# Set attention and a 2048-wide hard-swish layer on one core: the layer as a pairwise quadratic form over 32 inducing points

## The chip, the cores and the metric

The kernel runs on one core of a Trainium2 chip. The metric is device time in microseconds from the first to the last instruction of the program, as the median of three runs. Engines are named as in the profile: PE is TensorE's products and PEld its weight loads, DVE is VectorE, ACT is ScalarE, POOL is GpSimd, SP is SyncE.

## What is computed

Four batches of 12480 tokens of 128 features, 32 inducing points, and a layer that is 2048 wide:

```
def mab(q, kv):
    s = scale * (q @ kv.transpose(0, 2, 1))
    s = s - s.max(-1, keepdims=True)
    a = np.exp(s)
    a /= a.sum(-1, keepdims=True) + 1e-09
    return a @ kv
h = mab(I, x)                 # I: the 32 inducing points; h: (4, 32, 128)
attn = mab(x, h)              # (4, 12480, 128), reshaped to (49920, 128)
h2 = attn @ w_in              # (49920, 2048)
g = h2 * np.clip(h2 + 3.0, 0.0, 6.0) / 6.0
out = g @ w_out               # (49920, 128)
```

Where no entry of `h2` is beyond 3 in size, the clip does nothing and `g` is `h2*h2/6 + h2/2`. Each row of `attn` is a mean of the 32 rows of `h` with weights `a` that sum to one. So the square part of `out` is a quadratic form in the 32 weights.

## The kernel before, in words

Tokens go in chunks of 512 (24 full ones and one of 192 per batch). Before the first batch, and then woven into the chunks of the batch ahead, **phase A** makes `h`: x is cast to bf16 by a DMA into DRAM (`xbf`, L135) and read back transposed (`xt`, L139); per group of four 128-token tiles the fp32 rows come in again (`xs`, L182), are cast to fp32r on VectorE (`xa_ring`, L193), scores are taken (`s1p`, L196), exponentiated on ScalarE (`a`, L203), and four products add to `Hnd` (L166).

A chunk then runs in steps. **S1a** takes the scores of tokens against `h` (`s2p`, L244) and their exponentials; **S1b** sums, inverts and scales them on VectorE (L275 to L282) and transposes them (`a2tp`, L307); **S1c** multiplies by `H_sb` (`otu`, L321) and makes an fp32r copy `OT` (ScalarE, L323) and a bf16 copy `OTb` (VectorE, L325). **S2** is the layer: the linear half as one product with a folded 128x128 matrix (`W_sb`, L334), and for each of 16 blocks of 128 hidden units a product `hp` (L354), a square, and a product that adds to `outTp` (L344). Ten of the squares are one ScalarE instruction (L361), six are a copy and a product on VectorE (L364, L365); the second product of a block runs three blocks behind the first.

**S3** copies `outTp` (L374), transposes it back (`fp`, L387), copies it out of PSUM (L389, L391) and stores it (L394, L402). The order of the work comes from the order of the code, from `hooks` that put S1b, S1c, S3 and phase A of the next batch between the blocks j of S2, and from the buffers of the pools. x, weights and results move on SP's queue, the DMA cast on POOL's, `w_out` on ACT's.

## Time and profile before

| | |
|---|---|
| median of 3 runs | 1231.09 us (1230.43 to 1231.32) |
| span of the profiled execution | 1230.7 us, 0.4 us under the median |
| PE busy | 1034.0 us, 84% of the span |
| DVE busy | 844.4 us, 69% |
| ACT busy | 701.1 us, 57% |
| POOL busy | 6.7 us, 1% |
| moved by DMA | 79.86 MB, 65 GB/s over the span |
| granted TensorE clock | 0.962 of full, over the span |

The profiled execution has its span as its own time. A busy time is the union of an engine's instructions over the whole span, so it mixes the stages: the first 92 us, in which x and the weights arrive, the first aggregation up to about 162 us, and four batches of about 267 us each. What a stage is bound by is read from that stage alone. PE's products are pipelined: each record lasts longer than the distance to the next start, and the distance is what the engine spends.

### The profile page before, as it was taken

The page shows a single profiled execution, that of the slowest core. Times are in us where ns is not written, and L with a number is a line of the kernel's source. Part 1 is how long each engine was busy: PE and PEld are TensorE (multiplying, and loading weights), DVE is VectorE, ACT ScalarE, POOL GpSimd, SP SyncE. Part 2 cuts the span into 40 slices and gives each one's busy share as a digit, 9 for nine tenths or more (in the row PEclk, how much of TensorE's full clock was granted, in tenths as well). Part 3 has the DMA queues.
Part 4 walks back from the last instruction along what each step waited for, and adds up shares of the span by engine and source line. Part 5 has one row for each costly group of instructions (what it writes and reads, how often), then busy time and mean ns, then how long its engine had stood idle before and what let it go on. Part 6 is the DMA issues. An engine that isn't in the chain of part 4 may idle for free.

```text
span 1230.7 us, 16661 instructions
## 1 busy us (share of the span) xinstructions
PE 1034.0 (84%) x5413; PEld 455.1 (37%) x5413; DVE 844.4 (69%) x2342; ACT 701.1 (57%) x1614; POOL 6.7 (1%) x18
## 2 busy tenths in 40 slices
PE   0034699999999899999999799999999899999997
PEld 0033334444434434344434344334444333333333
DVE  0112578777778677788777677778876677777776
ACT  0011266666666466666666466666667466666665
POOL 2000000000000000000000000000000000000000
PEclk9995599999999899999999899999999899999999
DMA  9997311112113411112114311112110000000001
GB/s 229 218 226 182 98 35 44 52 52 60 43 47 82 112 44 43 52 44 61 52 47 109 76 44 52 48 48 60 44 38 26 14 25 26 27 26 27 20 25 38
DMA packets 155238, 79.86 MB, mean 65 GB/s; under 512 B 53872, under 2 KB 153744, under 8 KB 154256
## 3 DMA queue, kind: packets, MB, share of 16 engines
q1 hardware_dynamic: 153664, 64.98, 19.5%
q0 software_dynamic: 960, 12.78, 4.9%
q8 instruction: 42, 0.69, 0.3%
q10 hardware_dynamic: 528, 1.05, 0.2%
q14 instruction: 44, 0.36, 0.1%
HBM read 53.23 MB, written 38.34 MB: 74 GB/s over the span
## 4 chain that ended last, share of the span: by engine, by line
PE 45%; DVE 26%; issue 13%; DMA 7%; ACT 4%; SPq 4%; ACTq 0%; DVEq 0%; POOL 0%; POOLq 0%
PE outTp L344 21%; DVE u L364 16%; PE hp L354 16%; DVE q L365 7%; DMA xbf<-in_x_dram 4%; ACT q L361 4%; SPq L139 4%; PE otu L321 3%; DMA xs<-in_x_dram 2%; PE a2tp L307 2%; DVE rr L275 1%; PE fp L387 1%; DVE ri L281 1%; DMA out_dram<-ostage 1%; DVE xa_ring L193 0%
## 5 line engine op out<-in xcount | busy, mean ns | idle before, releaser
L354 PE MATMUL hp<-OTb,w_in_bf 128*128 128x512 bf16 (+1 forms) x1600 | 570.4, 379 | 46.9 <-DVE u L364 36.5
L361 ACT ACTIVATE q<-hp 128x512 bf16<-128x512 f32 (+1 forms) x1000 | 533.3, 618 | 89.7 <-PE hp L354 81.0
L344 PE MATMUL outTp<-q,w_bf 128*128 128x512 bf16 (+1 forms) x1600 | 549.3, 375 | 12.6
L364 DVE CAST u<-hp 128x512 bf16<-128x512 f32 x600 | 387.6, 666 | 14.4 <-PE hp L354 14.4
L365 DVE TENSOR_TENSOR q<-u 128x512 bf16<-128x512 bf16 x600 | 221.7, 408 | 0.8
L344 PEld LDWEIGHTS <-w_bf 128*128 128x128 bf16 x1600 | 141.6, 98 | 167.8 <-issue 91.0
L354 PEld LDWEIGHTS <-w_in_bf 128*128 128x128 bf16 x1600 | 145.9, 97 | 146.2 <-issue 91.0
L389 DVE COPY ostage<-fp 128x128 f32<-128x128 f32 x196 | 55.0, 281 | 181.4 <-PE fp L387 175.5
L323 ACT CAST OT<-otu 128x512 fp32r<-128x512 f32 (+1 forms) x100 | 57.5, 575 | 198.7 <-PE otu L321 198.7
L387 PE MATMUL fp<-ident_r,oT 128*128 128x128 f32 x392 | 126.2, 322 | 16.3 <-DVE ostage L389 5.0
L203 ACT ACTIVATE a<-s1p 128x128 fp32r<-128x128 f32 x96 | 26.6, 277 | 175.6 <-PE s1p L196 143.6
L166 PE MATMUL Hnd<-xa_ring,a 128*32 128x130 f32 x392 | 88.5, 312 | 31.3 <-DVE xa_ring L193 30.1
L325 DVE CAST OTb<-otu 128x512 bf16<-128x512 f32 (+1 forms) x100 | 67.6, 676 | 64.0 <-ACT OT L323 63.8
L193 DVE CAST xa_ring<-xs 128x128 fp32r<-128x128 f32 x392 | 61.3, 212 | 72.5 <-DMA xs<-in_x_dram 69.7
L387 PEld LDWEIGHTS fp<-ident_r,oT 128*128 128x128 f32 x392 | 54.6, 139 | 121.4 <-DVE ostage L389 46.2
L374 ACT CAST oT<-outTp 128x512 fp32r<-128x512 f32 (+1 forms) x100 | 57.5, 575 | 31.1 <-PE outTp L344 31.1
L391 ACT COPY ostage<-fp 128x128 f32<-128x128 f32 (+1 forms) x196 | 65.6, 335 | 8.8 <-PE fp L387 8.8
L313 DVE CAST a2t<-a2tp 32x512 fp32r<-32x512 f32 (+1 forms) x100 | 65.9, 659 | 0.0
L166 PEld LDWEIGHTS Hnd<-xa_ring,a 128*32 128x32 f32 x392 | 43.7, 116 | 52.0 <-DVE xa_ring L193 33.5
L196 PE MATMUL s1p<-I_T_bf,xt 128*128 128x32 bf16 x392 | 27.1, 183 | 34.3 <-DMA xt<-xbf 30.1
L334 PE MATMUL outTp<-OT,W_sb 128*128 128x512 f32 (+1 forms) x100 | 50.7, 507 | 2.4 <-ACT OT L323 1.6
L307 PEld LDWEIGHTS a2tp<-ident_r,a2n 128*32 128x32 f32 x392 | 25.3, 98 | 71.8 <-DVE a2n L282 65.2
(46 smaller groups left out, 351.1 us busy)
## 6 DMA issues: line engine op xcount, KB each, us to landing
xs<-in_x_dram SPq DMA_DIRECT2D x96, 256.0 KB, 2.9
out_dram<-ostage SPq DMA_DIRECT2D x96, 256.0 KB, 2.3
xbf<-in_x_dram POOLq DMA_DIRECT2D x12, 1040.0 KB, 37.1
w_in_f<-in_moe_w_in_dram SPq DMA_DIRECT2D x1, 1024.0 KB, 6.6
xs<-in_x_dram SPq DMA_DIRECT2D x4, 64.0 KB, 1.9
out_dram<-ostage SPq DMA_DIRECT2D x4, 64.0 KB, 2.3
xt<-xbf SPq DMA_TRANSPOSE x12, 7.5
xs<-in_x_dram SPq DMA_DIRECT2D x4, 32.0 KB, 2.0
```

The source lines that it names most:

```text
L166: nc.tensor.matmul(Hnd[:Mi, : C + 2], lhsT=p_a1[:rows, i * Mi : (i + 1) * Mi], rhs=xa_ring[:rows, slot, : C + 2], start=(t == 0), stop=(t ...
L193: nc.vector.tensor_copy(xa_ring[:rows, slot, :C], xs[:rows, i, :C])
L313: nc.vector.tensor_copy(a2t[:Mi, :ntok], a2tp[:Mi, :ntok])
L323: nc.scalar.copy(OT[:, :ntok], otu[:, :ntok])
L325: nc.vector.tensor_copy(OTb[:, :ntok], otu[:, :ntok])
L344: nc.tensor.matmul(outTp[:, :ntok], lhsT=w6_bf[:, j, :], rhs=qs[j][:, :ntok], start=False, stop=(j == FB - 1),)
L354: nc.tensor.matmul(hp[:, :ntok], lhsT=w_in_bf[:, j * P : (j + 1) * P], rhs=OTb[:, :ntok],)
L361: nc.scalar.activation(q[:, :ntok], hp[:, :ntok], ACT.Square)
L364: nc.vector.tensor_copy(u[:, :ntok], hp[:, :ntok])
L365: nc.vector.tensor_mul(q[:, :ntok], u[:, :ntok], u[:, :ntok])
L387: nc.tensor.transpose(fp[:rows, :C], oT[:, r0 : r0 + rows], ident_r[:, :])
L391: nc.scalar.copy(ostage[:rows, sl, :], fp[:rows, :C])
```

## The change

The whole kernel is written anew. With the clip inactive, the square part is rewritten with the identity that for weights of sum one the square of a mean is the mean of the squares less the sum over pairs of `a_i a_j (G_i - G_j)^2`, G being `w_in` applied to the rows of `h`. What is left per token is a product with 32 exact values of the layer at the inducing points, and one with a coefficient for each of the pairs; the products of exponentials `e_i e_j` are made as `exp` of sums of scores.

- A batch is cut into six groups of 2048 tokens and one of 192 (`groups`; 16 tokens to a partition, or 4 to each of 48 partitions), a group into chunks of 512 tokens. x is loaded as `xr` (fp32r) and, from the second batch on, again as `xb` (bf16), both on POOL's queue (`load_x`); in batch 0 VectorE and ScalarE cast it.
- **A** (`a_T`, `a_s1`, `a_agg`): transposes on TensorE through one PSUM buffer `pt`, scores, exponentials, `hnd` and the running sums `dacc`.
- **C** (`c_head` to `c_tail`), once a batch: `h` and its shifted sums and differences (`W`, `dH`), the layer at the inducing points (`c_G`, `c_L`, giving `BD`), and the pair coefficients `Cq` from 16 difference products and their squares (`c_sq`).
- **B**, per chunk: three base products and exponentials (`b_base`), three products of them on VectorE (`b_prod`), one fp32r and sixteen bf16 products into `op` (`b_out`), scaled by the squared inverse row sum into `os` (`b_evac`). Per group: `b_e`, `b_f`, `b_r` make the exponentials, the row sums and `r_all`.
- The order is the order of the code (`manual_schedule`): step t issues the base products of chunk t + 2 and the output of chunk t; A of the next batch is spread over the first 16 steps of a batch, C over the next six.
- At the end five counts test the largest `G`, the row sums and the sums of the weights; one number `bad_i` is loaded by every engine, and a branch goes to `direct_path`, which does the whole computation again token by token in 96-row tiles (three loops of 130 passes in each of four batches), or past it.

The diff, cut to what the steps below speak of (all functions shown above are taken out, `direct_path` is not shown):

```diff
-ACT_SQ_BLOCKS = 10
-MM2_DEPTH = 3
...
+        psF = es.enter_context(tc.tile_pool(name="psF", bufs=3, space=PSUM))
+        psO = es.enter_context(tc.tile_pool(name="psO", bufs=2, space=PSUM))
+        psX = es.enter_context(tc.tile_pool(name="psX", bufs=1, space=PSUM))
+        psS = es.enter_context(tc.tile_pool(name="psS", bufs=1, space=PSUM))
+        psH = es.enter_context(tc.tile_pool(name="psH", bufs=1, space=PSUM))
...
+        def load_x(b, g):
+            t0, p, n = groups[g]
+            src = x[b, t0 : t0 + p * n, :].rearrange("(p i) c -> p i c", i=n)
+            t = xin.tile([P, TG, C], FP32R, name="xr")
+            nc.gpsimd.dma_start(t[:p, :n, :], src)
+            xs[(b, g)] = t
+            if b > 0:
+                tb = xbin.tile([P, TG, C], BF16, name="xb")
+                nc.gpsimd.dma_start(tb[:p, :n, :], src)
+                xbs[(b, g)] = tb
...
+            pt = psX.tile([P, 1024], BF16, name="pt")
+            for i in range(lo, hi):
+                nc.tensor.transpose(pt[:, (i - lo) * p : (i - lo + 1) * p], xb[:p, i, :], ident_b[:p, :p])
+            nc.vector.tensor_copy(st["xT"][:, t0 + lo * p : t0 + hi * p], pt[:, : (hi - lo) * p])
...
+            s1 = psS.tile([P, 512], FP32, name="s1", tag="s1")
+            for i in range(n):
+                nc.tensor.matmul(
+                    s1[:p, i * M : (i + 1) * M],
+                    lhsT=st["xT"][:, t0 + i * p : t0 + (i + 1) * p],
+                    rhs=I_T[:, :],
+                )
+            a1 = a1p.tile([P, TG * M], FP32R, name="a1")
+            nc.scalar.activation(a1[:p, : n * M], s1[:p, : n * M], ACT.Exp, scale=scale)
...
+                nc.tensor.matmul(
+                    st["hnd"][:M, :C],
+                    lhsT=a1[:p, i * M : (i + 1) * M],
+                    rhs=xs[(b, g)][:p, i, :],
+                    start=(g == 0 and i == 0),
...
+                ahead = 3 if b == 0 else 2
+                if g + ahead < NGR:
+                    load_x(b, g + ahead)
...
+            dps = psF.tile([P, 512], FP32, name="dps", tag="fb")
+            nc.tensor.matmul(dps[:M, :2], lhsT=dred[:, :], rhs=ones[:, :2])
+            nc.vector.tensor_copy(d_all[:M, b : b + 1], dps[:M, :1])
...
+            gp = psF.tile([P, 512], FP32, name="gp", tag="fb")
+            for jb in range(FB):
+                nc.tensor.matmul(
+                    gp[:, jb * M : (jb + 1) * M],
+                    lhsT=w_in_r[:, jb * P : (jb + 1) * P],
+                    rhs=st["HTr"][:, :],
+                )
+            r6 = cst.tile([P, 512], FP32, name="r6")
+            nc.vector.tensor_scalar(r6[:, :], gp[:, :], 3.0, 0.0, op0=ALU.add, op1=ALU.max)
+            hs = cst.tile([P, FB, M], FP32R, name="hs")
+            nc.vector.scalar_tensor_tensor(
+                hs[:, :, :].rearrange("p a m -> p (a m)"), r6[:, :], 6.0, gp[:, :], op0=ALU.min, op1=ALU.mult
+            )
+            nc.vector.tensor_reduce(
+                g_all[:, b : b + 1], gp[:, :], axis=AX.X, op=ALU.max, apply_absolute_value=True
+            )
...
+                dpm = psF.tile([P, 512], FP32, name="dpm", tag="fb")
+                nc.tensor.matmul(
+                    dpm[:, :],
+                    lhsT=w_in_b[:, jb * P : (jb + 1) * P],
+                    rhs=st["dH"][:, :, :, :].rearrange("p k i m -> p (k i m)"),
+                )
+                sq = sqp.tile([P, 512], BF16, name="sq")
+                nc.scalar.activation(sq[:, :], dpm[:, :], ACT.Square)
...
+            for k in range(4):
+                nc.tensor.matmul(
+                    st["cp"][:, k * C : (k + 1) * C],
+                    lhsT=sq[:, k * P : (k + 1) * P],
+                    rhs=w6n[:, jc, :],
...
+            ep = psF.tile([P, 512], FP32, name="ep", tag="fb")
+            for s in range(SL):
+                rhs = st["xT"][:, t0 : t0 + n * p].rearrange("c (j s p) -> c s j p", s=SL, p=p)[:, s]
+                nc.tensor.matmul(
+                    ep[32 * s : 32 * s + 32, : J * p], lhsT=st["HTb"][:, :], rhs=rhs,
+                    tile_position=(0, 32 * s),
+                )
+            e = efp.tile([P, 512], FP32R, name="e")
+            nc.scalar.activation(e[:, : J * p], ep[:, : J * p], ACT.Exp, scale=scale)
...
+            sp = psF.tile([P, 512], FP32, name="sp", tag="fb")
+            nc.tensor.matmul(sp[:, : J * p], lhsT=blk[:, :], rhs=e[:, : J * p])
+            nf = efp.tile([P, 512], FP32R, name="nf")
+            nc.vector.tensor_tensor_reduce(
...
+            rp = psF.tile([P, 512], FP32, name="rp", tag="fb")
+            for j in range(J):
+                nc.tensor.matmul(
+                    rp[:p, j * SL : (j + 1) * SL], lhsT=nf[:, j * p : (j + 1) * p], rhs=one4[:, :]
+                )
+            c0 = first_chunk[g]
+            nc.vector.reciprocal(
+                r_all[:p, b, c0 : c0 + J, :].rearrange("p j s -> p (j s)"), rp[:p, : J * SL]
+            )
...
+            for k in range(3):
+                bp = psF.tile([P, 512], FP32, name="bp", tag="fb")
+                nc.tensor.matmul(
+                    bp[:, :w],
+                    lhsT=st["W"][:, k].rearrange("p i m -> p (i m)"),
+                    rhs=st["xT"][:, c0 : c0 + w],
+                )
+                pool = tp if k == 0 else dp
+                t = pool.tile([P, 512], BF16, name=f"x{k}")
+                nc.scalar.activation(t[:, :w], bp[:, :w], ACT.Exp, scale=scale)
+                ex.append(t)
+            return ex, w
...
+            nc.vector.tensor_mul(T1[:, :w], T0[:, :w], D1[:, :w])
+            nc.vector.tensor_mul(T2[:, :w], T0[:, :w], D2[:, :w])
+            nc.vector.tensor_mul(T3[:, :w], T2[:, :w], D1[:, :w])
...
+            nc.tensor.matmul(
+                op[:p, :],
+                lhsT=st[("nf", g)][:, j * p : (j + 1) * p],
+                rhs=st["BD"][:, :],
...
+            for s in range(SL):
+                for k in range(4):
+                    nc.tensor.matmul(
+                        op[:p, s * C : (s + 1) * C],
+                        lhsT=T[k][:, s * p : (s + 1) * p],
+                        rhs=st["Cq"][:, k, :],
...
+            nc.vector.tensor_mul(
+                ot[:p, j * SL : (j + 1) * SL, :],
+                op[:p, :].rearrange("p (s c) -> p s c", c=C),
+                r_all[:p, b, c, :].unsqueeze(2).to_broadcast([p, SL, C]),
+            )
...
+        for t in range(-LEAD - 2, total):
+            if t >= 0 and t % NCK == 0:
+                b = t // NCK
...
+                    steps_a = NCK - LEAD - 2 - C_LEN + 1
+                    per = [len(queue) * (i + 1) // steps_a - len(queue) * i // steps_a for i in range(steps_a)]
+                    cq = c_pieces(b + 1)
+                    for i in range(C_LEN):
+                        per.append(len(cq) * (i + 1) // C_LEN - len(cq) * i // C_LEN)
+                    queue += cq
...
+            for a in evac:
+                b_evac(*a)
+            evac = []
+            tb = t + LEAD
+            if 0 <= tb < total:
+                bb, cc = divmod(tb, NCK)
+                ex, w = b_base(bb, cc)
+            for (b, g) in at_e.get(t, []):
+                b_e(b, g)
+            for (b, g) in at_f.get(t, []):
+                b_f(b, g)
+            for (b, g) in at_r.get(t, []):
+                b_r(b, g)
+            if t >= 0:
+                k = t % NCK
+                for _ in range(per[k] if k < len(per) else 0):
+                    queue.pop(0)()
+            if 0 <= tb < total:
+                b_prod(bb, cc, ex, w)
+            if t >= 0:
+                bo, co = divmod(t, NCK)
+                evac.append((bo, co, b_out(bo, co)))
...
+        nc.vector.tensor_scalar(
+            junk[:, :NR], r_all[:, :, :, :].rearrange("p b c s -> p (b c s)"), 1.0e-16, None,
+            op0=ALU.is_ge, op1=ALU.add, accum_out=cnt[:, 0:1],
+        )
...
+        nc.tensor.matmul(cp5[:1, :5], lhsT=ones[:, 0:1], rhs=cnt[:, :])
+        cs = cst.tile([1, 1], FP32, name="cs")
+        nc.vector.tensor_reduce(cs[:, :], cp5[:1, :5], axis=AX.X, op=ALU.add)
+        good = float(P * (NR + B * NGR + 3 * B))
+        nc.vector.tensor_scalar(bad_i[:, :], cs[:, :], good, None, op0=ALU.not_equal)
...
+    bad = nc.values_load(
+        bad_i[0:1, 0:1], min_val=0, max_val=1, skip_runtime_bounds_check_because="a comparison gives 0 or 1"
+    )
+    with tc.If(bad > 0):
+        direct_path(tc, x, inducing, moe_w_in, moe_w_out, out, scale)
...
```

Three places show how the engines' orders differ. On TensorE, before, in the middle of a chunk (`w_bf` and `w_in_bf` are the two weight matrices in bf16, `fp` the transposed result of an earlier chunk):

```order
L344 LDWEIGHTS w_bf
L344 MATMUL outTp<-q,w_bf 128x512
L387 MATMUL fp<-ident_r,oT 128x128
L354 LDWEIGHTS w_in_bf
L354 MATMUL hp<-OTb,w_in_bf 128x512
```

and now, in the middle of a batch, the end of one step's base products, the group's `rp`, and the first of the sixteen output products (`x_2270` is the first exponential, the `T_` tiles the three products, `Cq` the pair coefficients):

```order
L454 LDWEIGHTS W
L454 MATMUL bp<-xT,W 128x512
L437 MATMUL rp<-one_143,nf 128x4 x4
L481 MATMUL op<-BD_159,nf 128x512
L491 LDWEIGHTS x_2270
L491 MATMUL op<-Cq,x_2270 128x128
L491 LDWEIGHTS T_2310
L491 MATMUL op<-Cq,T_2310 128x128
L491 LDWEIGHTS T_2311
L491 MATMUL op<-Cq,T_2311 128x128
L491 LDWEIGHTS T_2312
L491 MATMUL op<-Cq,T_2312 128x128
```

The 512-column products with fixed weights are followed by 128-column products, each of which loads token data as its weights.

On VectorE, before, in a chunk in which the next batch's aggregation runs:

```order
L364 CAST u<-hp 128x512
L282 TENSOR_TENSOR a2n<-a2u,ri 128x128
L365 TENSOR_TENSOR q<-u 128x512 x2
L313 COPY a2t<-a2tp 32x512
L389 CAST ostage<-fp 128x128
L193 CAST xa_ring<-xs 128x128 x4
L325 CAST OTb<-otu 128x512
```

and now, in a step of the same kind (`pt` holds transposed x, `dacc` the running sums, `op` the output of the chunk before):

```order
L189 COPY xT<-pt 128x1024
L221 TENSOR_TENSOR dacc<-dacc,a_2711 128x512
L470 TENSOR_TENSOR T_2777<-x_2741,x_2745 128x512
L471 TENSOR_TENSOR T_2778<-x_2741,x_2749 128x512
L472 TENSOR_TENSOR T_2779<-T_2778,x_2745 128x512
L508 TENSOR_TENSOR os<-op,r_all 128x512
L418 ISA nf,nf_all<-e,sp 128x512
L418 ISA nf_all 128x1
```

The copies and squares of the hidden layer are gone; three products of exponentials stand behind the copies that A needs.

On POOL, before, from the identity matrix on:

```order
masks.py:197 MEMSET ident 128x128
L135 DMA xbf<-in_x_dram 64x8320
masks.py:199 ISA
masks.py:199 AFFINE_SELECT ident<-ident 128x128
L135 DMA xbf<-in_x_dram 64x8320 x11
```

and now, at the same place:

```order
masks.py:199 AFFINE_SELECT ident<-ident 128x128
L107 DMA xr<-in_x_dram 128x2048 x3
L107 DMA xr<-in_x_dram 48x512
L156 DMA w_in_r<-in_moe_w_in_dram 128x2048
L157 DMA w_out_r<-in_moe_w_out_dram 128x16x128
L107 DMA xr<-in_x_dram 128x2048
L111 DMA xb<-in_x_dram 128x2048
```

All loads of x, and both weight matrices, are now issued by POOL, behind one another.

## Rows read from the trace of the kernel before

**Rows 1.** The page, busy time and instructions of each engine.

```profile
PE 1034.0 (84%) x5413; PEld 455.1 (37%) x5413; DVE 844.4 (69%) x2342; ACT 701.1 (57%) x1614; POOL 6.7 (1%) x18
```

**Rows 2.** Windows: start:end, length, busy us of each engine, clock, DMA share, GB/s.

```profile
0.00:92.00 92.00, 12.60 (x93) 10.87 (x93) 8.59 (x42) 4.79 (x16) 6.74 (x18) 0.97 1.02 224
92.00:162.00 70.00, 40.27 (x248) 23.23 (x249) 33.11 (x142) 16.21 (x44) 0.00 (x0) 0.60 0.49 124
162.00:430.00 268.00, 247.63 (x1326) 108.80 (x1325) 205.12 (x571) 171.54 (x395) 0.00 (x0) 0.98 0.22 61
```

**Rows 3.** The page, the chain that ended last, shares of the span by engine.

```profile
PE 45%; DVE 26%; issue 13%; DMA 7%; ACT 4%; SPq 4%; ACTq 0%; DVEq 0%; POOL 0%; POOLq 0%
```

**Rows 4.** Groups by shape: hidden layer; busy us, mean ns, idle before, releasers.

```profile
L354 PE MATMUL hp<-OTb,w_in_bf 128*128 128x512 bf16 x1536 | 557.6, 385 | 46.9 <-DVE u L364 36.5
L344 PE MATMUL outTp<-q,w_bf 128*128 128x512 bf16 x1536 | 537.6, 381 | 12.4
L361 ACT ACTIVATE q<-hp 128x512 bf16<-128x512 f32 x960 | 522.4, 629 | 87.3 <-PE hp L354 80.2
L364 DVE CAST u<-hp 128x512 bf16<-128x512 f32 x576 | 379.9, 680 | 14.4 <-PE hp L354 14.4
L365 DVE TENSOR_TENSOR q<-u 128x512 bf16<-128x512 bf16 x576 | 216.0, 415 | 0.0
```

**Rows 5.** Timeline, TensorE: start us, us busy, engine, line, operation, count.

```profile
74.21 0.27 PEld L196 LDWEIGHTS <-xt 128*128 128x128 bf16 x4
...
75.97 0.72 PE L166 MATMUL Hnd<-xa_ring,a 128*32 128x130 f32 x4 [1.38 <-DVE xa_ring L193]
...
702.53 0.50 PE L334 MATMUL outTp<-OT,W_sb 128*128 128x512 f32 x1
702.88 0.39 PE L344 MATMUL outTp<-q,w_bf 128*128 128x512 bf16 x1
...
708.01 0.38 PE L354 MATMUL hp<-OTb,w_in_bf 128*128 128x512 bf16 x1
...
708.22 0.38 PE L344 MATMUL outTp<-q,w_bf 128*128 128x512 bf16 x1
...
1224.40 0.25 PE L344 MATMUL outTp<-q,w_bf 128*128 128x192 bf16 x1
1224.48 0.25 PE L354 MATMUL hp<-OTb,w_in_bf 128*128 128x192 bf16 x1
```

**Rows 6.** Groups by shape: an fp32r weight load and a small reciprocal.

```profile
L387 PEld LDWEIGHTS fp<-ident_r,oT 128*128 128x128 f32 x388 | 54.2, 140 | 115.9 <-DVE ostage L389 40.7 <-ACT ostage L391 29.3 <-ACT a L203 28.0
L281 DVE RECIPROCAL ri<-rr 128x4 f32<-128x4 f32 x96 | 15.8, 165 | 0.1
```

**Rows 7.** Timeline: runs of like instructions on VectorE and ScalarE.

```profile
705.16 1.27 DVE L364 CAST u<-hp 128x512 bf16<-128x512 f32 x2
...
706.30 3.54 ACT L361 ACTIVATE q<-hp 128x512 bf16<-128x512 f32 x7
...
706.36 0.74 DVE L365 TENSOR_TENSOR q<-u 128x512 bf16<-128x512 bf16 x2
```

**Rows 8.** The page, DMA issues: count, KB each, median us from issue to landing.

```profile
out_dram<-ostage SPq DMA_DIRECT2D x96, 256.0 KB, 2.3
xbf<-in_x_dram POOLq DMA_DIRECT2D x12, 1040.0 KB, 37.1
w_in_f<-in_moe_w_in_dram SPq DMA_DIRECT2D x1, 1024.0 KB, 6.6
```

**Rows 9.** Timeline: the last instructions before the span ends.

```profile
1227.36 1.09 SPq L402 DMA_DIRECT2D out_dram<-ostage  x2
...
1227.67 0.26 ACT L391 COPY ostage<-fp 64x128 f32<-64x128 f32 x1 [1.00 <-PE fp L387]
```

More of the change, by code (lines that the diff above doesn't have):

```diff
@@ L42 @@
     B, N, C = x.shape
-    Mi = inducing.shape[0]
+    M = inducing.shape[0]
     F = moe_w_in.shape[1]
     FB = F // P
-    assert C == P and Mi <= P and F % P == 0
+    assert C == P and M == 32 and FB == 16
     scale = 1.0 / math.sqrt(C)
-    NT = (N + P - 1) // P
-    NCH = (N + CHUNK - 1) // CHUNK
-    NG = (NT + GROUP - 1) // GROUP
-    assert N % 16 == 0, "token count must be a multiple of 16 for the DMA transpose"
-    xt_piece = XT_PIECE if N % XT_PIECE == 0 else N
-    assert N % xt_piece == 0 and xt_piece % 16 == 0
@@ L265, in S1b @@
-    def S1b(b, ch):
-        c, ct0, ntok = ch
-        d = st[(b, c)]
-        nsl = d["nsl"]
-        a2u = d["a2u"]
-        rr = a2pool.tile([P, 4], FP32, name="rr")
-        ri = a2pool.tile([P, 4], FP32, name="ri")
-        a2n = a2pool.tile([P, 4 * Mi], FP32R, name="a2n")
-        full = (nsl == 4) and (ntok == CHUNK)
-        if full:
+    groups = []
+    t0 = 0
+    while N - t0 >= P * TG:
+        groups.append((t0, P, TG))
+        t0 += P * TG
+    rest = N - t0
+    if rest:
+        assert rest % SL == 0 and rest // SL <= P and (rest // SL) % 2 == 0
+        groups.append((t0, rest // SL, SL))
@@ new lines, in c_L @@
+        def c_L(b):
+            st = S[b]
+            lp = psF.tile([P, 512], FP32, name="lp", tag="fb")
+            for jb in range(FB):
+                nc.tensor.matmul(
+                    lp[:, :M],
+                    lhsT=w_out_r[:, jb, :],
+                    rhs=st["hs"][:, jb, :],
+                    start=(jb == 0),
+                    stop=(jb == FB - 1),
+                )
+            LT = cst.tile([P, 4, M], FP32, name="LT")
+            nc.vector.tensor_scalar_mul(
+                LT[:, :, :], lp[:, :M].unsqueeze(1).to_broadcast([P, 4, M]), -1.0 / 6.0
+            )
+            lt = psF.tile([P, 512], FP32, name="lt", tag="fb")
+            nc.tensor.transpose(lt[:, :C], LT[:, :, :].rearrange("p q m -> p (q m)"), ident[:, :])
+            bd = BD[b % 2]
+            for q in range(4):
+                nc.vector.tensor_copy(
+                    bd[32 * q : 32 * q + 32, q * C : (q + 1) * C], lt[32 * q : 32 * q + 32, :C]
+                )
+            st["BD"] = bd
@@ L282, in S1b, with b_evac @@
+        def b_evac(b, c, op):
+            g, j = chunks[c]
+            t0, p, n = groups[g]
+            st = S[b]
+            if j == 0:
+                st["os"] = osp.tile([P, TG, C], FP32, name="os")
+            ot = st["os"]
             nc.vector.tensor_mul(
[L283 to L302 removed]
@@ new lines @@
+        C_LEN = 6
+        queue = []
+        prod = None
+        for t in range(-LEAD - 2, total):
+            if t >= 0 and t % NCK == 0:
+                b = t // NCK
+                if b + 1 < B:
+                    for g in range(2):
+                        load_x(b + 1, g)
+                    a_begin(b + 1)
+                    queue = a_pieces(b + 1)
+                    steps_a = NCK - LEAD - 2 - C_LEN + 1
[4 more added lines that the diff above has]
+                    queue += cq
+                else:
+                    per = []
+            for a in evac:
+                b_evac(*a)
+            evac = []
+            tb = t + LEAD
[17 more added lines that the diff above has]
+                evac.append((bo, co, b_out(bo, co)))
```

785 lines of the change are left out of this document (410 added, 375 removed).

## The prediction

> **What bounds the kernel now.** I read the busy table first, then the span cut into stages, the chain that ended last, the groups of instructions by shape, and last the start times inside dense stretches. The busy table names TensorE: 1034.0 of 1230.7 us, VectorE next with 844.4, ScalarE 701.1 [rows 1]. The stages show where: 92 us in which the DMA engines are the busy ones and TensorE works for 12.6; 70 us in which batch 0 is aggregated at a granted clock of 0.60; and then four batches of some 267 us each (the first of them 162 to 430), where TensorE is busy 247.6 of 268 at a clock of 0.98, VectorE 205.1, ScalarE 171.5 [rows 2]. The chain agrees: 45% TensorE, 26% VectorE [rows 3]. Inside a batch the hidden layer is nearly all of it: 3200 products of 128 columns by 512 tokens (1536 full ones on each of L354 and L344, the rest the short chunks), which ScalarE and VectorE square in between [rows 4]. Those products start 0.21 us apart where they run dense (708.01, 708.22), though each shows 0.38 [rows 5]; I cost by start distances, not durations. 100 chunks x 32 x 0.215 = 688 us of TensorE's stream is this layer. So a change that removes it changes the bound itself.
>
> **What is removed.** Per chunk, 32 products at 0.215 (6.9 us), ten squarings on ScalarE, six copies and six squarings on VectorE, four fp32 transposes and the x cast on VectorE. All of it lay on or just beside the path; nothing of the old sum remains, so I sum the new program from its start, not as a difference.
>
> **What one chunk costs now (TensorE).** Three base products (512 columns) 3 x 0.215 = 0.65. One fp32r product of 512 columns (`nf` by `BD`): 702.53 to 702.88 = 0.35, taken 0.34 [rows 5]. Sixteen bf16 products of 128 columns, each with its own 128x128 weights. No such row exists. Lower bound 0.055, a 192-column pair (1224.40 to 1224.48: 0.083) scaled by columns; upper bound 0.083 itself. Four 32-column pairs load in 0.27, one load lasting 0.10, so a pair can be as short as 0.056 [rows 5]; nearest to the lower end, I take 0.06: 0.96. A quarter of a group's share: `ep`, four 32-row products into different column strips, 0.215 if they run side by side, 0.86 in turn; the nearest row is a single 512-column product, so 0.86; `sp` 0.34; `rp`, four fp32r weight loads at 0.14 [rows 6] (upper end 0.34), 0.56; together 1.76 / 4 = 0.44. Sum 2.39.
> One wait comes on top. `ep`, `sp`, `rp` take a buffer of the three-deep `psF` ring that the step's three base products have just filled; it is free when ScalarE has done the first exponential, 0.22 + 0.17 drain + 0.55 = 0.94 us into the step, while TensorE is there at 0.65. With the hand-over that is 0.35 in three of four steps, 0.26 a step. So 2.65 us for a chunk without other work.
>
> **The next batch's aggregation (A).** A group of 2048 tokens: 16 transposes at 0.06, 16 scores at 0.06, 16 fp32r products of 128 columns at 0.137 (four of 130 columns in 0.72, one 0.31: 75.97) [rows 5]: 4.1 us. 6.1 groups a batch = 25 us, laid on the first 16 steps only: 1.57 a step. 2.65 + 1.57 = 4.22.
>
> **What lies beside it.** VectorE per step: three bf16 products at 0.37 (two in 0.74), the final product from PSUM 0.66 (between 0.64 and 0.68), `nf` and the reciprocal (0.68 + 0.17) / 4; A adds two 1024-wide copies and one addition a group. A two-byte PSUM copy has no row: 0.74 at best (the rate of the bf16 product), 1.27 at worst (two 512-wide PSUM copies) [rows 6, 7]. At the worst: 1.98 + (2.54 + 0.66) x 6.1 / 16 = 3.2 against 4.22. ScalarE: three exponentials at 0.51 (seven squarings in 3.54) [rows 7] + shares 0.33 = 1.86. Both have cover; if TensorE's step fell under 3.2, VectorE would be next. DMA: per batch 6.4 MB in fp32, 3.2 MB in bf16, 6.4 MB out; at the 224 GB/s of the first stretch [rows 2] 71 us of a batch of 109. The transfers are issued two or three groups ahead and wait for buffers only, not for the step; POOL runs nothing else. I cost them at nothing; uncovered they would set 71 us a batch, still less than TensorE.
>
> **The coefficients of the next batch (C)** fall into six steps. TensorE's part: 32 fp32r weight loads at 0.14 = 4.5, 16 x 0.215 = 3.4, 64 x 0.06 = 3.8, small ones 1: 12.7. Own work of the steps 6 x 2.39 = 14.3. And three hand-overs in which TensorE, in order, waits for VectorE: sum, reciprocal, H and its transpose (about 2); the buffer of `gp`, which three 512-wide VectorE passes must read first (2.4); `LT` and its transpose (1.5). Together 33. ScalarE's 16 squarings are 8.2 and fit.
>
> **Start and end.** First x group: one 1 MB load lands in 6.6 us and the first pieces of the old cast took longer (median 37.1, several in flight) [rows 8]; I take 8. Six groups at 6.5: the trace shows this stage at a granted clock of 0.60 [rows 2], that is mostly 1.2 of 2.4 GHz, so transposes 16 x 0.107, scores 0.9, aggregation 2.2, and 1.7 for the copies between two transposes of one PSUM buffer; the DMA alone would give 1.05 MB / 224 GB/s = 4.7. With the short group 2: 49 us. C alone 22 (head 5.6, G 4.5, squarings 8.2, L and tail 3.7). Lead-in steps 7. Start 78. The end: five counts, a product, a compare, the last store and the branch; the old kernel needed 2.8 us from its last 0.26 us copy (1227.67) to the span's end [rows 9], and I add four for the count chain and the register load: 7.
>
> **Sum.** 78 + 3 x (16 x 4.22 + 33 + 3 x 2.65) + 25 x 2.65 + 7 = 78 + 326 + 66 + 7 = 477. This is a span; the old span is 1230.7, its median of runs 1231.09, 0.4 more, which rounds away here.
>
> The term of 0.06 carries most. The Trainium skill (TensorE: Matmul & The Clock Gate, Back-to-back issue gap) gives a sustained 81 ns for a pair at N = 128, and 131 ns at N = 512. The trace contradicts its second figure (0.21 at 512 columns) and cannot rule on the first in a long run. By 81 ns the sum would be an estimated 527.
>
> **Rivals.**
> 1. Pairs cost 0.083, as at 192 columns. 1600 out products, 586 transposes and scores, 192 in C: 2378 x 0.023 = 55, 532 us. For: no row shows more than four short pairs in a run. Against: those four. The skill's 81 ns would be this case.
> 2. VectorE's queue decides. Its products for chunk t+2 stand behind the A copies, which wait for transposes late in the step. If the queue falls more than a step behind, TensorE waits for T tiles: A steps 5.2 instead of 4.22 (+48 over 48 steps), C +15, the other 34 steps +0.3 (10): 550 us. For: VectorE at 3.2 of 4.22 with in-order waits. Against: the lead of two chunks.
> 3. Hand-overs vanish: `ep` side by side (-16), no `psF` wait (-21), C in 27 (-18), start groups nearer the DMA floor (-11): 411 us.
> 4. Slower: the test fails and the branch is taken. It decides at L603, where a count that differs from 56320 by one sends all engines into three loops of 130 passes per batch. A pass holds at least a load, 2.3 us to land even for a store of this kind [rows 8], and some ten dependent steps: 1560 x 3 to 10 us = 4.7 to 16 ms on top. The reference's inputs speak against it: the largest |w_in x H| that I work out from them is 0.0037 against the limit 3, row sums lie at 32, and the counts are small whole numbers that fp32 holds exactly. That the change does not do what it says is the same rival.
>
> **Chances.** Forecast 0.49, pairs 0.22, VectorE 0.15, faster rival 0.12, branch taken 0.02. The range 410 to 565 takes in the first four; outside are the low half of rival 3, some joint cases of rivals 1 and 2, and the branch. 0.2% (2.5 us, about what can be told from no change) is far from all: faster 0.98, same 0.00, slower 0.02.
>
> **What would show it.** Step 1: products of 128 columns starting 0.06 apart. Step 2: chunk period 4.2 with A, 2.65 in the last batch, TensorE over 85% busy there and waits on ScalarE's exponentials at `ep`, `sp`, `rp`. Step 3: C's six steps 33 us. Step 4: the first base product of batch 0 near 75 us. Step 5: no wait for `xb` or `xr` after the start. It is wrong if VectorE ends the waits of the `op` products (rival 2), if starts lie 0.08 apart (rival 1), or if lines of the direct path appear.

## The result, and the profile after

The changed kernel takes 439.03 us as the median of 4 runs (433.88 to 445.99), against 1231.2 us before (1230.43 to 1233.28): a ratio of 0.3539, 95% interval [0.3523, 0.3555]. The forecast was 477 in a range of 410 to 565: the side and the range hold, and the middle was 38 us too high. The ratios leave out disturbed runs, so they need not be the quotients of the medians, and the rows below are from a second profiled execution of the same kernel, the control of the experiments (436.9 us median, span 435.0), since the first profile fell in such a run.

The first lines of its page: span, TensorE's busy time, the chain that ended last.

```profile
span 435.0 us, 9390 instructions
PE 362.9 (83%) x3907; PEld 262.6 (60%) x3907; DVE 286.6 (66%) x707; ACT 224.0 (51%) x429; POOL 29.4 (7%) x57
PE 62%; ACT 14%; DMA 10%; DVE 8%; issue 3%; POOL 1%; ACTq 0%; POOLq 0%
```

TensorE still has the largest share, as in [rows 1] and [rows 3], but of a third of the time. 671 of its 1034 busy microseconds are gone.

The same execution by stage: A of batch 0, C and the lead-in, then cut at the first output product of each batch and at the last output (busy time of each engine, then granted clock, DMA share, GB/s):

```profile
0.00:41.00 41.00, 23.37 (x301) 20.85 (x301) 20.71 (x49) 13.04 (x16) 9.36 (x20) 0.87 0.81 236
41.00:61.00 20.00, 17.04 (x120) 12.42 (x120) 6.64 (x23) 8.91 (x17) 0.41 (x1) 0.68 0.50 153
61.00:68.60 7.60, 5.34 (x38) 2.49 (x38) 4.94 (x12) 5.68 (x11) 0.00 (x0) 1.00 0.00 1
68.60:165.40 96.80, 86.05 (x980) 62.09 (x978) 68.96 (x167) 53.48 (x105) 7.44 (x14) 0.98 0.56 167
165.40:269.20 103.80, 90.95 (x981) 65.59 (x978) 69.27 (x167) 53.48 (x105) 7.42 (x14) 0.93 0.53 155
269.20:366.30 97.10, 87.78 (x965) 63.54 (x961) 68.17 (x166) 52.30 (x104) 4.72 (x9) 0.95 0.39 119
366.30:421.65 55.35, 50.80 (x525) 34.50 (x522) 45.17 (x111) 37.08 (x74) 0.00 (x0) 1.00 0.26 104
421.65:435.00 13.35, 1.62 (x23) 1.12 (x20) 2.75 (x14) 0.00 (x0) 0.00 (x0) 0.66 0.24 93
```

Row by row this is the forecast's sum:

| term | forecast | measured | difference |
|---|---|---|---|
| start (A of batch 0, C, lead-in) | 78 = 49 + 22 + 7 | 68.6 = 41 + 20 + 7.6 | -9.4 |
| three batches | 3 x 108.5 = 326 | 96.8 + 103.8 + 97.1 = 297.7 | -28 |
| last batch, 25 steps | 66 | 55.4 | -11 |
| end | 7 | 13.4 | +6 |
| sum | 477 | 435.0 | -42 |

The last batch's row holds 24 steps, up to the start of the last output; that output stands in the row of the end.

TensorE's records in the last batch, where only chunk work runs (start, length, instruction, idle time before it and its releaser):

```profile
365.96 0.40 PE L402 MATMUL ep<-xT,HTb 128*32 128x512 bf16 x4 [0.25 <-ACT x L461]
366.29 0.49 PE L481 MATMUL op<-BD,nf 128*128 128x512 f32 x1
...
368.60 0.50 PE L416 MATMUL sp<-e,blk 128*128 128x512 f32 x1 [0.26 <-ACT x L461]
368.94 0.40 PE L481 MATMUL op<-BD,nf 128*128 128x512 f32 x1
...
371.14 0.38 PE L454 MATMUL bp<-xT,W 128*128 128x512 bf16 x1 [0.47 <-ACT x L461]
371.17 0.69 PE L437 MATMUL rp<-one,nf 128*128 128x4 f32 x4
371.72 0.47 PE L481 MATMUL op<-BD,nf 128*128 128x512 f32 x1
...
372.94 0.81 PE L454 MATMUL bp<-xT,W 128*128 128x512 bf16 x3
373.40 0.58 PE L481 MATMUL op<-BD,nf 128*128 128x512 f32 x1
373.83 0.23 PE L491 MATMUL op<-Cq,x 128*128 128x128 bf16 x1
...
374.73 0.59 PE L454 MATMUL bp<-xT,W 128*128 128x512 bf16 x2
```

The step that starts at 372.94 waits for nothing. Its base products and `op` take 0.89 (forecast 0.65 + 0.34), its sixteen pair products 373.83 to 374.73 = 0.90, or 0.056 each (forecast 0.06). `ep` costs 0.33 (365.96 to 366.29), `sp` 0.34, `rp` 0.55. The three bracketed waits are for an exponential of L461 that frees a `psF` bank.

What TensorE and its weight loads waited for in that batch (total us, times, longest), of the kernel after:

```profile
PE sp L416 <- ACT x L461: 1.5, 6, 0.3
PE ep L402 <- ACT x L461: 1.5, 6, 0.3
PE rp L437 <- ACT x L461: 1.3, 5, 0.3
PE bp L454 <- ACT x L461: 0.5, 1, 0.5
...
PEld sp L416 <- ACT x L461: 4.5, 6, 0.7
...
PEld rp L437 <- ACT x L461: 3.5, 5, 0.8
```

Of what waits here for another engine, nearly all is the wait that the forecast put at 0.26 a step.

### The profile page after: what moved, and what is told of

The parts are those of the page before. It is cut to its first block, busy times and chain, and to the rows that moved or that the text cites. A ratio compares the mean times of both kernels' runs of the same rounds, so it can differ in the third digit from the quotient of the medians.

```text
span 438.8 us, 9376 instructions
## 1 busy us (share of the span) xinstructions
PE 362.4 (83%) x3893; PEld 263.9 (60%) x3907; DVE 287.3 (65%) x707; ACT 224.0 (51%) x429; POOL 29.4 (7%) x57
## 4 chain that ended last, share of the span: by engine, by line
PE 62%; ACT 13%; DMA 10%; DVE 8%; issue 3%; POOL 1%; ACTq 0%; POOLq 0%
PE op L491 20%; ACT x L461 10%; DMA xb<-in_x_dram 8%; PE bp L454 7%; PE op L481 7%; PE pt L188 5%; PE hnd L210 4%; PE dpm L349 3%; PE rp L437 3%; PE sp L416 3%; PE cp L364 3%; DMA xr<-in_x_dram 2%; PE gp L305 2%; ACT sq L355 2%; DVE os L508 2%
## 5 line engine op out<-in xcount | busy, mean ns | idle before, releaser
L461 ACT ACTIVATE x<-bp 128x512 bf16<-128x512 f32 x300 | 154.4, 588 | 145.5 <-PE bp L454 133.8
L491 PE MATMUL op<-Cq,T 128*128 128x128 bf16 (+1 forms) x1200 | 105.0, 225 | 0.0
L491 PE MATMUL op<-Cq,x 128*128 128x128 bf16 (+1 forms) x400 | 91.0, 228 | 0.0
L491 PEld LDWEIGHTS <-T 128*128 128x128 bf16 (+1 forms) x1200 | 87.7, 101 | 0.0
L508 DVE TENSOR_TENSOR os<-op,r_all 128x512 f32<-128x512 f32 (+1 forms) x100 | 68.7, 687 | 22.9 <-PE op L491 22.5
L454 PE MATMUL bp<-xT,W 128*128 128x512 bf16 (+1 forms) x288 | 80.9, 384 | 1.7 <-ACT x L461 0.5
L491 PEld LDWEIGHTS <-x 128*128 128x128 bf16 (+1 forms) x400 | 40.3, 101 | 18.0 <-issue 12.8
L481 PE MATMUL op<-BD,nf 128*128 128x512 f32 (+1 forms) x100 | 49.3, 493 | 0.0
L470 DVE TENSOR_TENSOR T<-x,x 128x512 bf16<-128x512 bf16 (+1 forms) x100 | 40.6, 406 | 7.9 <-ACT x L461 7.0
L472 DVE TENSOR_TENSOR T<-T,x 128x512 bf16<-128x512 bf16 (+1 forms) x100 | 41.8, 418 | 3.4
L471 DVE TENSOR_TENSOR T<-x,x 128x512 bf16<-128x512 bf16 (+1 forms) x100 | 41.2, 412 | 1.3
```

The source lines that it names most:

```text
L454: nc.tensor.matmul(bp[:, :w], lhsT=st["W"][:, k].rearrange("p i m -> p (i m)"), rhs=st["xT"][:, c0 : c0 + w],)
L461: nc.scalar.activation(t[:, :w], bp[:, :w], ACT.Exp, scale=scale)
L470: nc.vector.tensor_mul(T1[:, :w], T0[:, :w], D1[:, :w])
L471: nc.vector.tensor_mul(T2[:, :w], T0[:, :w], D2[:, :w])
L472: nc.vector.tensor_mul(T3[:, :w], T2[:, :w], D1[:, :w])
L481: nc.tensor.matmul(op[:p, :], lhsT=st[("nf", g)][:, j * p : (j + 1) * p], rhs=st["BD"][:, :], start=True, stop=False, skip_group_check=True,)
```

## The experiments

Each kernel ran beside the kernel before on its chip; ratios are to that. The three theories under test: the group products wait for PSUM banks; the `xb` load and the hand-overs in C stall TensorE; the end is the branch's. Their rivals: VectorE's queue sets the steps, or a wait that is taken away comes back at the next late thing.

**Control.** No edit.

> The changed kernel again, for a same-chip comparison with the next three. Theory T (TensorE's stream sets the time; on top come a hand-over at the first PSUM ring, a late bf16 load of x, and the end of the program): 434 to 446 us as in its first runs. Rival R (VectorE's queue sets it) expects the same here; the run only fixes the level.

436.9 us (434.6 to 440.01), ratio 0.3551 [0.353, 0.3571].

**No branch.** The register load, the branch and `direct_path` are left out; the counts and `bad_i` stay.

```diff
-    bad = nc.values_load(bad_i[0:1, 0:1], ...)
-    with tc.If(bad > 0):
-        direct_path(tc, x, inducing, moe_w_in, moe_w_out, out, scale)
```

> Leaves out the load of the test's result, the branch and the direct path behind it; the five counts stay. Theory: of the 9.4 us between the issue of the last store (429.4) and the end of the span, about 2 are the store's landing and about 7 are the register load, the branch and the jump past the direct path; so 6 to 8 us less than the control, and the stretch behind the last store shrinks to 2 to 3 us. Rival: the stretch is the store and the program's own end, as any kernel has it; then under 1 us less.

425.55 us (423.89 to 429.24), ratio 0.3451 [0.3441, 0.3462]. The medians differ by 11.4 us, more than the end does. Other stretches vary between executions (in this profile the start took 71.1 us against 68.6, the second batch 98.2 against 103.8), and what the rest of the difference is was not tried; the end is read from the trace. The last VectorE record, `os` for the last 48 rows, in the timeline of the control (span 435.0):

```profile
424.52 0.67 DVE L508 TENSOR_TENSOR os<-op,r_all 48x512 f32<-48x512 f32 x1
```

and in that of this kernel (span 427.5):

```profile
423.68 0.67 DVE L508 TENSOR_TENSOR os<-op,r_all 48x512 f32<-48x512 f32 x1
```

From its end to the end of the span: 9.8 us with the branch, 3.1 without (the kernel before: 2.8, [rows 9]). The branch, never taken, costs 6.7 us.

**Short body.** The load and the branch stay, the body is one memset instead of `direct_path`.

```diff
     with tc.If(bad > 0):
-        direct_path(tc, x, inducing, moe_w_in, moe_w_out, out, scale)
+        # one memset of a small tile
```

> The test's result is still loaded and branched on, but behind the branch stands one small memset instead of the direct path. Taking all of it out shortened the stretch from the last output product to the end from 13.4 to 6.7 us. If the price is the register load and the compare, this one keeps it: 13 us again, level with the control (435 to 440). If it is the jump past a long body and what the program's end does with it, the stretch falls to 7 to 9 us.

434.02 us (432.16 to 435.3), ratio 0.3522 [0.351, 0.3534]. The same record (span 432.6):

```profile
426.09 0.67 DVE L508 TENSOR_TENSOR os<-op,r_all 48x512 f32<-48x512 f32 x1
```

426.76 to 432.6 = 5.8. So of the 6.7 us about 2.7 come with the load and the branch, whatever the body, and 4.0 depend on the code that is skipped. The traces show where both lie (sequencer's records: number, shortest, median and longest in ns, first and last start). In the control, then with the short body:

```profile
L611 PEldq COMPARE_BRANCH  x1: 3657/3657/3657, 425.8 to 425.8; - x1
```

```profile
L611 PEldq COMPARE_BRANCH  x1: 219/219/219, 427.4 to 427.4; - x1
```

With the long body the branch takes 3.66 us of TensorE's queue instead of 0.22, and the other engines have no record from 426.2 to 429.6. In that gap five packets of the instruction queues move, and five more right behind it; with the short body there are none. That the fetching of code takes the time fits this but is not shown. The 2.7: in both kernels POOL's last long record, a drain of 4.2 us, starts only behind the branch (429.9 and 427.5); without a branch it starts at 303.2, beside other work.

**`xb` first.** The bf16 load is issued ahead of the fp32r load of the same group.

```diff
+            if b > 0:
+                tb = xbin.tile([P, TG, C], BF16, name="xb")
+                nc.gpsimd.dma_start(tb[:p, :n, :], src)
             t = xin.tile([P, TG, C], FP32R, name="xr")
             nc.gpsimd.dma_start(t[:p, :n, :], src)
-            (the same three lines, behind xr)
```

> Only the order of two transfers on POOL's queue is swapped: the bf16 copy of a group is issued before its fp32r copy. Theory: in the trace xb lands 12.7 us after its issue because the 1 MB of xr goes ahead of it; it would land 3 to 5 us earlier, the 2.4 us wait of the transposes at 104.5 goes, and with it the 10 us at half clock that follow; batches 1 and 2 fall from 102 and 101 us to 95 to 98, 8 to 15 us in all. Rival: the queue's rate is the limit (both copies are needed soon), then xr is late in xb's place and the time stays within 2 us.

429.79 us (428.45 to 430.95), ratio 0.3488 [0.3477, 0.3499]: 7 us less than the control, and under half of its spread (2.5 against 5.4). In the second batch of the control the timeline has

```profile
203.41 0.62 PE L188 MATMUL pt<-ident_b,xb 128*128 128x128 bf16 x8 [2.10 <-DMA xb<-in_x_dram]
```

and its DMA issues from 190 to 206 (engine, KB, median us to landing):

```profile
xr<-in_x_dram POOLq DMA_DIRECT2D x1, 1024.0 KB, 7.7
out_dram<-os SPq DMA_DIRECT2D x1, 1024.0 KB, 11.3
xb<-in_x_dram POOLq DMA_DIRECT2D x1, 512.0 KB, 12.3
```

The half-size load lands last, behind 1 MB on its own queue. Issued first it lands in 5.6 (185 to 206 of this kernel; over all 18 such loads the median falls from 9.6 to 5.4), no product waits for `xb`, and the two steps of 6.34 and 4.42 us become 4.07 and 2.78. Between the two profiles the gain is the second batch's alone, 103.8 to 96.7 us; the other two stay within 0.5. The half clock (granted 0.50, that is 1.2 of 2.4 GHz) that followed the wait, from 204 to 207.5 us, is gone too; 10 us of it in C of the third batch are still there.

**Group products last.** `b_e`, `b_f`, `b_r` of a step stand behind its output products.

```diff
-            (the three loops over at_e, at_f, at_r, behind b_base)
...
                 evac.append((bo, co, b_out(bo, co)))
+            (the same three loops here)
```

> The per-group work (ep, sp, rp) moves from right behind the three base products to the end of the step, behind the output products. Theory T: its wait for the first exponential (a step with it takes 2.65 to 2.73 us in the last batch, one without 1.68, and its own products are worth 0.2 to 0.5) goes, 0.4 to 0.6 us in 75 steps: 25 to 45 us less. Rival R (VectorE's queue sets the step): under 8 us less. A second rival: the wait moves to the third base product, which then needs the buffer that ep holds, and half the gain goes: 10 to 20 us.

444.01 us (440.07 to 447.97): no gain, in its best run either. The last batch is 53.8 us (55.4), its steps 2.55, 2.72, 2.26, 1.79 instead of 2.65, 2.67, 1.68, 2.73. `ep`, `sp` and `rp` wait no longer; in their place, in that batch, stand

```profile
PE bp L454 <- ACT x L461: 3.1, 7, 0.5
...
PEld op L481 <- DVE T L472: 5.5, 9, 0.8
```

The group products now hold a bank when the next base products come, and these wait for it; `op` waits for the third VectorE product instead. The ring is what is short, and its wait moves with the order.

**Two products.** The third VectorE product is left out (T3 is T2, so a quarter of the pair products read T2 in its place).

```diff
-            T3 = tp.tile([P, 512], BF16, name="T3")
...
-            nc.vector.tensor_mul(T3[:, :w], T2[:, :w], D1[:, :w])
+            T3 = T2
```

> Leaves out the third of VectorE's three products per chunk (the second stands in for it in the output); TensorE does all that it did. 0.42 us x 100 = 42 us of VectorE's work go. Theory T: 0 to 8 us less. Theory R: 20 us less or more.

436.0 us (434.23 to 440.49), ratio 0.3533 [0.3525, 0.354]. Last-batch steps 2.65, 2.68, 1.68, 2.72, those of the control. With 0.42 of some 1.8 us less on VectorE a step nothing moves: VectorE's queue does not set the steps.

**Both of these.** Group products last and the third product left out.

> The group work at the end of the step, as in the run before (444 us, no gain), and the third VectorE product left out as well. Mixed theory M: with the ring's wait gone VectorE's queue fell behind and took the gain back (output products there wait for the third product); without that product the last batch's steps fall from an average of 2.33 to about 2.0 us, and the time is 15 to 35 us under that run, more than the third product gives alone. Against it: if the gain was lost to the late loads and the coefficient steps only, the last batch stays at 2.3 a step and the time within 8 us.

439.67 us (429.6 to 441.19); last batch 52.8 us, steps 2.55, 2.60, 2.26, 1.79. The wait of `op` for VectorE's third product is gone, the steps stay, and the mixed theory falls with them: the base products still wait for the banks of `ep` and `sp`, and the weight loads stand 13 us under "issue", for which the trace names no cause. The 429.6 is one run of four, the others took 439 to 441; the profile is one of those.

**Half the pairs.** Eight of the sixteen output products are left out.

```diff
-                for k in range(4):
+                for k in range(2):
```

> Leaves out half of the output's pair products: 8 instead of 16 products of 128 columns per chunk (k = 0 and 1 only); VectorE, ScalarE and the transfers do all that they did. Theory T (TensorE's stream sets the step): 8 x 0.057 x 100 = 46 us less, a little less where the waits take some: 35 to 46. Theory R (VectorE's queue sets it): under 15 us less.

417.33 us (410.49 to 427.72), ratio 0.3389 [0.3365, 0.3412]. 20 us less by the medians: under the 35 to 46 of one theory, over the 15 of the other. In most steps with A the price is confirmed: they get 0.45 shorter (3.47 to 3.02), which is 8 x 0.056. But 100 x 0.45 = 45 us became 26 in span (408.7 against 435.0). In the last batch the steps fall from 2.65, 2.67, 1.68, 2.73 to 2.20, 2.34, 1.86, 2.28, which is 0.26 a step and not 0.45. There VectorE is busy nine tenths of the time (the five busy times as above, VectorE's the third):

```profile
356.00:390.00 34.00, 28.21 (x226) 16.46 (x223) 30.67 (x75) 27.02 (x51) 0.00 (x0) 1.00 0.29 117
```

and the weight loads of `op` and `rp` wait for its products for 6.2 us, against 1.7 in the control: with less TensorE work VectorE's queue comes next. Another part is the granted clock: over the batches this run has 34 us of half clock, the control 27 (summed from the windows view in pieces of 2 us, a piece at 0.50 counting 2 us), some of it in the last batch, where the control has none: there three steps are 4.48, 2.79 and 3.40 instead of 2.34, 1.86 and 2.28. Less TensorE work between the same waits was followed by a lower clock. Its products wait 9.1 us for `xb`, the control's 3.1; an exact split was not made.

**A bank for the group products.** `ep`, `sp`, `rp` get their own PSUM bank; the output gives one of its two.

```diff
-        psO = ...(name="psO", bufs=2, space=PSUM)
+        psO = ...(name="psO", bufs=1, space=PSUM)
+        psG = ...(name="psG", bufs=1, space=PSUM)
...
-            ep = psF.tile([P, 512], FP32, name="ep", tag="fb")
+            ep = psG.tile([P, 512], FP32, name="ep", tag="g")
```

(and `sp`, `rp` alike)

> Chunk B's products ep, sp and rp get a PSUM bank of their own in place of turns in the two banks that the base products rotate through; the output pool pays for it with one buffer instead of two. Nothing is left out. Theory F (two thirds of a last-batch step's waits are TensorE waiting for a base-product bank): the waits of 0.5 to 0.65 us in three of four steps go, the last batch of 25 steps falls from 55.4 us to 45 to 48 us, and the whole to 400 to 417 us. Rival W (the wait only moves, as it did when the group products were put last): last batch within 2 us of 55.4, the whole within 5 us of the control. Rival O (the single output buffer is now what TensorE waits for): last batch above 58 us and the whole slower by 10 us or more.

437.36 us (431.69 to 438.05), ratio 0.3539 [0.3514, 0.3565], last batch 57.3. The waits for L461 are gone, and in their place, from the same view of that batch:

```profile
PEld op L482 <- DVE os L509: 11.7, 24, 1.0
```

Steps with A in them become 0.5 shorter (3.47 to 2.94), last-batch steps even out at 2.34 and 2.47, each waiting for the one output bank. Rival W holds, for the last batch and for the whole. The bank decides, but this edit only moved the shortage; the last experiment below gives both.

**Head of C in pieces.** `xb` first, and `c_head` cut in three at its waits (`dred`; `dps` to `H`; `htp` to `dH`), in three steps, with C over seven steps.

```diff
-            ps = [lambda: c_head(b), lambda: c_G(b)]
+                [lambda: c_h1(b)],
+                [lambda: c_h2(b)],
+                [lambda: c_h3(b), lambda: c_G(b)],
...
-        C_LEN = 6
+        C_LEN = 7
```

> Transfer order of e2 (inducing-block load ahead of the rounded one), and the head of stage C cut into three pieces that are put into three chunk steps, so that C takes 7 steps instead of 6 and its serial products stand between chunk A and B work. Nothing is left out. Theory I (TensorE's idle in C's head and the stretch at half clock behind it cost 5 to 12 us a batch): batches of about 97 us become 89 to 94, the whole 410 to 422 us against 429.8 for the transfer order alone, and no row of granted clock near 0.5 stands behind C's head. Rival N (the chain's waits only move into the steps that follow): within 3 us of 429.8.

427.76 us (424.97 to 430.07), ratio 0.3482 [0.3467, 0.3497], which overlaps that of `xb` first. The half clock over the batches fell from 20 to 10 us, but batches are 95.8, 96.9 and 92.6 us (97.3, 96.7, 97.0): five of the seven steps of C take 4.4 to 6.5 us in the new places too. The rival holds by the time, 2 us by the medians. The head's waits in a batch, 0.5 us for `dred` and 0.9 for `H`, became one of 1.0 for `HTr`, at the products that follow.

**Both, with one output bank.**

> The two edits before together: transfer order, head of C in three pieces, a bank of their own for ep, sp and rp. Nothing is left out. If the two work on different waits the gains add: 385 to 405 us. If both only shift the same wait, within 4 us of the better of the two alone.

422.32 us (418.39 to 473.47), ratio 0.3431 [0.3415, 0.3448]. 5 us better than the split head alone, and far from the 385 to 405 of gains that add. The steps with A are some 15 us shorter over the three batches; the step behind C in each (3.95 instead of 2.26 us) and the last batch, again 57.4 us, take 7 of it back.

**And a second output bank in the last batch.** There the score bank of A is idle, and takes every second output tile.

```diff
-            op = psO.tile([P, 512], FP32, name="op")
+            if b == B - 1 and c % 2:
+                op = psS.tile([P, 512], FP32, name="op", tag="s1")
+            else:
+                op = psO.tile([P, 512], FP32, name="op")
```

> The three edits together (transfer order, head of C in three pieces, own bank for ep, sp and rp), and in the last batch, where stage A's score products no longer run, every second output tile lies in the bank that they leave free, so that there the output has two banks again and the group products keep their own. Nothing is left out. Theory F (the waits of a last-batch step are for PSUM banks, in turn those of the base products and, with one output bank, that of the output): 24 last-batch steps without either take 2.0 us each, 46 to 50 us against 55.4 in the control and 57.4 with one output bank, and the whole is 411 to 416 us against 422. Rival W (the waits move on, to the next thing that is late): last batch 53 to 56 us, the whole 417 to 421 us. The busy time of VectorE in that stretch, 45 us, is the floor under both.

409.39 us (407.85 to 412.1), ratio 0.3322 [0.3313, 0.333]. The last batch is 47.7 us, inside the 46 to 50 of the theory, and TensorE is busy in all of it:

```profile
349.30:397.00 47.70, 47.70 (x525) 34.98 (x521) 44.28 (x110) 37.37 (x74) 0.00 (x0) 1.00 0.30 121
```

Its products wait for nothing any more; its weight loads (L417 is `ep`, L499 and L509 the output's) for this:

```profile
PEld L509 <- issue: 4.4, 21, 0.3
PEld L417 <- issue: 2.1, 5, 0.4
PEld op L499 <- issue: 0.9, 4, 0.2
PEld op L499 <- DVE os L526: 0.4, 2, 0.2
```

and the step that waited 0.47 at 371.14 above runs through (timeline of TensorE):

```profile
360.98 0.81 PE L469 MATMUL bp<-xT,W 128*128 128x512 bf16 x3
361.44 0.69 PE L452 MATMUL rp<-one,nf 128*128 128x4 f32 x4
361.99 0.48 PE L499 MATMUL op<-BD,nf 128*128 128x512 f32 x1
```

This is the fastest version of the study: it computes the same as the changed kernel, in 27 us less than the control.

## Why the prediction was right, and where its steps were off

**Step 1, the pair products: right.** 0.056 us a pair in runs of sixteen with fresh weights, forecast 0.06, and half of them taken away gave 0.45 back in most steps with A. Rival 1 (0.083) falls. The Trainium skill (TensorE: Matmul & The Clock Gate, Back-to-back issue gap) gives a sustained 81 ns at N = 128 and 131 at N = 512; here a long run shows 0.056, and 512-column products stood 0.21 apart before. The measurement decides against both; the gap of an isolated product in the same section of the Trainium skill, 56 and 216 ns, is what the stream shows.

**Step 2, a chunk: right in its parts, each a little dear.** The average last-batch step is (2.65 + 2.67 + 1.68 + 2.73) / 4 = 2.43, forecast 2.65. Own work is 0.89 + 0.90 = 1.79, plus a quarter of `ep` 0.33 + `sp` 0.34 + `rp` 0.55, so 2.10, and the steps of the last kernel, where no product waits, average 2.09. (The split is less sure than the sum: there a step with `ep` is 0.52 longer than one without, `sp` 0.24, `rp` 0.45.) The forecast had 2.39: `ep` in turn (0.86) was the wrong end, its four products run side by side; the rest came from rounding each price up. The wait was there as described, 0.33 a step instead of 0.26, and taking it away brought 55.4 - 47.7 = 7.7 us, 0.32 in each of 24 steps. Rival 3 was half right: `ep` is side by side, the `psF` wait is not gone.

**A: mis-sized.** 1.57 a step was forecast. The control's timeline shows what the pieces cost at full clock:

```profile
103.25 0.65 PE L210 MATMUL hnd<-xr,a 128*32 128x128 f32 x8
103.73 0.57 PE L196 MATMUL s<-I_T,xT 128*128 128x32 bf16 x16
104.15 0.61 PE L188 MATMUL pt<-ident_b,xb 128*128 128x128 bf16 x8
104.57 0.48 PE L481 MATMUL op<-BD,nf 128*128 128x512 f32 x1
```

Eight aggregation products take 0.48, 0.060 each and not 0.137; sixteen scores 0.42, 0.026 each and not 0.06; eight transposes 0.42. A group is 16 x (0.060 + 0.026 + 0.053) = 2.2 us instead of 4.1, so 0.85 a step. The scores have 32 columns and were priced like 128. The 0.137 came from four products behind a wait of 1.38 us [rows 5], at a granted clock of 1.00 like these; why those four stood twice as far apart was not tried.
Not all of this arrived. In a step the piece of A or C stands ahead of the output, so a distance between two outputs holds the piece of the later step, and the first piece of A falls into the lead-in. The 47 distances with A take 171.6 us, 3.65 each, forecast 4.22 (198.3): that is 27 of the 28 us of the table, 10 of it the chunk's (47 x 0.22) and 16 A's. C takes 4 us more than forecast, the steps without either 3.5 less. A is worth 3.65 - 2.43 = 1.22 a step, so nearly 0.4 a step is not its own work. Part of it are waits that the forecast had not: in each batch 1.2 us for the exponential of the scores and 0.8 for the copy of `pt`, and over the whole run 3.1 for `xb`. The rest was not traced.

**C: right in size, by errors that cancel.** 33 was forecast; the six steps of the three batches take 32.5, 35.4 and 35.2:

```profile
121.40:153.90 32.50, 27.79 (x255) 19.26 (x254) 18.79 (x52) 18.77 (x37) 0.53 (x1) 0.95 0.39 131
222.30:257.70 35.40, 30.80 (x256) 21.44 (x254) 18.82 (x52) 18.89 (x37) 0.53 (x1) 0.86 0.36 118
321.50:356.70 35.20, 30.70 (x257) 21.64 (x255) 18.77 (x52) 18.78 (x37) 0.00 (x0) 0.85 0.15 61
```

TensorE is idle for 4.5 to 4.7 of them, where the hand-overs were put at 5.9, and the chunks' own work is 6 x 2.10, 1.7 less than thought. On the other side stands time at half clock that the forecast did not have: the two batches with a mean granted clock of 0.86 and 0.85 take 2.8 us longer than the one with 0.95.

**What lies beside it: one claim wrong.** "The transfers are issued two or three groups ahead and wait for buffers only" was the reason to cost them at nothing. In place of that, `xb` stands behind `xr` on its queue, landed after 12.3 us in the second batch, and TensorE waited. The change of order is worth 7 us. VectorE has cover, as said (rival 2 falls with the run of two products); the copy of `pt` took 0.69, less than both ends of its range (0.74 and 1.27):

```profile
L189 DVE COPY xT<-pt 128x1024 bf16<-128x1024 bf16 x48 | 33.1, 689 | 30.8 <-PE pt L188 30.6
```

**Start: 9.4 us too dear, end: 6.4 too cheap.** A of batch 0 took 41 us against 49: the granted clock is 0.87 where 0.60 was taken over from the old stage. The DMA engines are busy there at a share of 0.81 and move 236 GB/s, so the load may set this stretch; no run tried it. In the end the four microseconds added for the count chain and the load were the mis-sized term: the branch with its long body costs 6.7. From the start of the last chunk's output to the end of its `os` another 3.5 pass, over 1 us of it because VectorE does the counts first: TensorE's last product ends at 423.1, `os` starts at 424.52. Rival 4 did not happen: no line of `direct_path` ran.

## What to carry to other kernels

Take the price of an operation from rows of its own shape in a long run: four products behind a wait, and 128 columns in place of 32, nearly doubled the term of A here. When several tile kinds share a ring of PSUM banks, moving the code moves the wait: count the banks that each stretch of the program leaves idle and lend them there. A load that is needed first is issued first on its queue, whatever its size.

## What the runs showed of the hardware that was not expected

- A branch whose body never runs cost 6.7 us at the end, 4.0 of them only with a long body behind it (9.8, 5.8 and 3.1 us from the last VectorE record to the end of the span). With the long body the branch itself took 3.66 us of TensorE's queue, with the short one 0.22.
- Four products of 512 columns with 32 stationary columns each, in four column strips, cost 0.33 us together by their starts, and made a step 0.52 longer in the last kernel, where one of 128 stationary columns costs 0.21. fp32r products of 128 columns on 32 stationary ones cost 0.060 each in runs of eight.
- A 0.5 MB load with a cast, behind 1 MB on the same queue, landed after 12.3 us in one place, with a 1 MB store under way as well; ahead of it, after 5.6. Medians over the run: 9.6 and 5.4.
- In the control the granted clock fell to 0.50 for stretches of 3 to 10 us in every batch with A and C work, but not in the last batch, where TensorE was busy 50.80 of 55.35 us. With half the pair products it fell there too.
